# Four-token sums of v on TensorE instead of a second load of v, sums of q on GpSimd, another written order

## The chip, the core and the metric

The kernel runs on one core of a Trainium2 chip. A core has a matrix engine (TensorE, PE in the profile, PEld for its weight loads), VectorE (DVE), ScalarE (ACT), GpSimd (POOL), a queue engine (SyncE, SP) that issues most DMAs, and 16 DMA engines. The metric is the device time of one execution in microseconds; the median of several runs counts.

## The reference

An attention of two parts over q, k, v of shape (8 batches, 8 heads, 576 tokens, 64), all fp32, is followed by a mixture of 8 experts with one expert per token. Cut to what matters:

```python
q_d = q.reshape(B, H, Sd, 4, D).mean(axis=3)      # the same for k_d and v_d; Sd = 144
out_up = np.repeat(sm_attn(q_d, k_d, v_d), 4, axis=2)
mask = np.abs(pos[:, None] - pos[None, :]) < 4
out_local = softmax(where(mask, q k^T / 8, -1e9)) @ v
x = (out_up + out_local) as (4608 tokens, 512)
e_idx = argmax(x @ w_gate + modality_bias[modality_id]); gate_w = its softmax value
out[t] = gate_w[t] * (relu(x[t] @ w1[e]) @ w2[e])
```

So v is needed twice: as it is, in windows around each query (local part), and summed over four tokens (the part here called downsampled).

## The kernel before

The attention works on pairs of heads: iteration n = 4 b + hp is batch b and pair hp, 32 iterations in all, two heads on the two halves of the 128 partitions. For each n, TensorE transposes q and k (`tpq`, `tpk`, `tpt`, all tagged "T" in a ring of three PSUM banks), ScalarE and VectorE copy them to `qT` and `kT`, and the four-token sums are made along the free dimension: k by two adds on GpSimd (`d`, `kd`), q by one reduction on VectorE (`qd`, L301). `sc` is the local scores (48 small matmuls of 24 queries by 32 keys, four side by side), `scd` the downsampled scores. VectorE takes maxima (`lm`, `dm`), ScalarE exponentiates (`exp`, `de`), GpSimd scales (`nl`, `nd`). The local weights are transposed on VectorE and placed in `Pw`; the downsampled ones are transposed on TensorE (`pdt`) with the 144 keys in two halves of 72, and copied to `PdT`. `avl` and `avd` multiply by v, and `X` adds both.

Two loads bring v. `load_v` fills `vw`, in which partition 32 j + x, column (head, k) holds token 96 k + 24 j - 3 + x, x from 0 to 31: windows of 32 tokens at a pitch of 24, for `avl`. `load_vg` (L237) brings the same v again, eight tokens to a partition, 288 KB for each n, into the expert stage's weight buffers (`raw`) for n below 28 and into q's and k's buffers after that; GpSimd's `vt` and `vd_` (L251, L258) add its tokens to `vd`, 72 keys by 2 halves.

After every batch the router multiplies x with the gate weights (`lg`), finds each token's expert, scatters token numbers into a table and stores the rows of x in HBM (`xr`, `R`, `store`). Two units of 256 tokens are computed early, in the attention's tail; then come the last router counts, tables, gathers of rows (`xg`, transposed by `xt`), and some 17 further units of expert matmuls (L844, L891).

The order of all instructions of the attention and the router is written out: `PHASE` gives each step a time in iterations, step f of iteration n gets n + PHASE[f], and the calls are sorted by it and issued in that order on every engine, each of which runs its own in order. Loads stand at times computed from PHASE. When the last scores are through (`free`, L1036), the buffers of q, k and their sums are given back, and the early experts' weights are split in them. Behind that a scheduler sets the order.

Of the kernel before, what the change touches and what calls it, by code (L numbers as in the profile page):

```python
# [75 lines left out]
class Consts:  # L76
    def __init__(s, tc, pool, psum):
        nc = tc.nc

# [12 lines left out]
        m = pool.tile([128, WIN], BF16, name="band")
        nc.gpsimd.memset(m, 0.0)
        for j in range(4):
            t = m[32 * j : 32 * j + 32]
# [2 lines left out]
            nc.gpsimd.affine_select(out=t, in_=t, pattern=[[-1, WIN]], compare_op=ALU.is_ge, fill=NEG, base=6,
                                    channel_multiplier=1)
# [81 lines left out]
class Attention:  # L181


    def __init__(s, tc, ctx, ectx, C, psum, raw, q, k, v):
        s.tc, s.C, s.ps, s.raw = tc, C, psum, raw
# [10 lines left out]
        for j in range(2):
            nc.vector.memset(s.kT[j][:, 0:PAD], 0.0)
            nc.vector.memset(s.kT[j][:, S + PAD :], 0.0)
            nc.vector.memset(s.vw[j][0:32, 0], 0.0)
            nc.vector.memset(s.vw[j][96:128, H * NB - 1], 0.0)  # L200

        for j in range(NPW):
            nc.gpsimd.memset(s.Pw[j], 0.0)
# [33 lines left out]
    def load_vg(s, n):  # L237
        b, hp = divmod(n, 4)
        if n < 28:
            vg = s.raw.tile([128, 1024], F32, name="raw")  # L240
        else:
# [4 lines left out]
    def vt(s, n, i):
        v5 = s.VG.pop(n).rearrange("p h (c t d) -> p (h c) t d", c=2, t=4)
        t = s.t["vt", n] = s.ld.tile([72, 4, 2, D], F32, name="vt", bufs=2)  # L250
        s.nc.gpsimd.tensor_tensor(t, v5[:, :, 0:2], v5[:, :, 2:4], op=ALU.add)  # L251

    def vd_(s, n, i):
        b, hp = divmod(n, 4)
        if hp == 0:
            s.vd[b] = s.wk.tile([72, H, 2, D], F32, name="vd")
        t = s.t.pop(("vt", n))
        s.nc.gpsimd.tensor_tensor(s.vd[b][:, 2 * hp : 2 * hp + 2].rearrange("p h c d -> p (h c) d"), t[:, :, 0],  # L258
                                  t[:, :, 1], op=ALU.add)
# [37 lines left out]

    def qd(s, n, i):

        dd = s.t["qd", n] = s.ld.tile([128, 144], F32, name="qd")  # L300
        s.nc.vector.tensor_reduce(dd, s.t["qT", n].rearrange("m (g t) -> m g t", t=4), op=ALU.add, axis=AX.X)  # L301

    def d(s, n, i):
        d2 = s.t["d", n] = s.ld.tile([128, 144, 2], F32, name="d2", bufs=1)
        T4 = s.kT[n % 2][:, PAD : PAD + S].rearrange("m (g t) -> m g t", t=4)
        s.nc.gpsimd.tensor_tensor(d2, T4[:, :, 0:2], T4[:, :, 2:4], op=ALU.add)

    def kd(s, n, i):
        d2 = s.t.pop(("d", n))
        dd = s.t["kd", n] = s.ld.tile([128, 144], F32, name="kd")  # L310
        s.nc.gpsimd.tensor_tensor(dd.rearrange("m (c g) -> m g c", c=2), d2[:, :, 0].rearrange("m (g c) -> m g c", c=2),
                                  d2[:, :, 1].rearrange("m (g c) -> m g c", c=2), op=ALU.add)
# [67 lines left out]
    def nd(s, n, i):  # L380
        z, e = s.t["zr", n], s.t["de", n]
        s.nc.gpsimd.tensor_tensor(e, e, z[:, 2 * NB :].unsqueeze(2).broadcast_to([128, 3, 144]), op=ALU.mult)
# [12 lines left out]
    def pdt(s, n, kc):  # L395

        p = s.t["pdt", n, kc] = s.ps.tile([72, 512], F32, name="pdt", tag="T", bufs=3)
        for c in range(3):
            s.nc.tensor.transpose(p[:, 128 * c : 128 * c + 128], s.t["de", n][:, c, 72 * kc : 72 * kc + 72], s.C.ident)
# [8 lines left out]
    def avd(s, n, i):  # L408
        b, hp = divmod(n, 4)
        PdT = s.t.pop(("PdT", n))  # L410
        pd = s.t["avd", n] = s.ps.tile([128, 144], F32, name="avd", tag="A", bufs=2)
        for kc in range(2):
            for a in range(2):
                s.nc.tensor.matmul(pd[64 * a : 64 * a + 64, :], s.vd[b][:, 2 * hp + a, kc, :], PdT[:, kc, a, :],
# [489 lines left out]
def build(tc, q, k, v, mid, w_gate, bias, w1, w2, out):  # L904
    nc = tc.nc
    with ExitStack() as ctx:
# [8 lines left out]
        with ExitStack() as actx:  # L915
# [47 lines left out]
            for nm, p in P.items():  # L963
# [199 lines left out]
```

## Time and profile before

| | |
|---|---|
| median of 3 runs | 773.27 us (770.15 to 775.43) |
| profiled run | 774.68 us, span 773.0 us |
| TensorE busy | 702.1 us, 91% of the span |
| VectorE, ScalarE, GpSimd busy | 473.6, 433.2, 327.3 us |
| granted TensorE clock, mean | 0.937 |
| moved by DMA | 150.97 MB |

The span falls into the attention (to about 310 us), a tail in which early experts run beside the last iterations, and the expert stage up to 773 us. In rows of instruction groups, "x" is followed by a count, then come the busy time in us, the mean length of one in ns, and the idle time of the engine just ahead of them with what ended it; "issue" there means that no wait in the profile explains it. In rows of waits stand the total in us, how often, and the longest. In rows of windows, each engine has its busy time and number of instructions, then come the granted clock as a share of the full one, the mean busy share of the DMA engines and GB/s. A matmul of fp32 data shows as two rows.

### The profile page before, as it was taken

The page shows a single profiled execution, that of the slowest core. Times are in us where ns is not written, and L with a number is a line of the kernel's source. Part 1 is how long each engine was busy: PE and PEld are TensorE (multiplying, and loading weights), DVE is VectorE, ACT ScalarE, POOL GpSimd, SP SyncE. Part 2 cuts the span into 40 slices and gives each one's busy share as a digit, 9 for nine tenths or more (in the row PEclk, how much of TensorE's full clock was granted, in tenths as well). Part 3 has the DMA queues.
Part 4 walks back from the last instruction along what each step waited for, and adds up shares of the span by engine and source line. Part 5 has one row for each costly group of instructions (what it writes and reads, how often), then busy time and mean ns, then how long its engine had stood idle before and what let it go on. Part 6 is the DMA issues. An engine that isn't in the chain of part 4 may idle for free. (4 is left out here: it accounts for less than half of the span.)

```text
span 773.0 us, 20639 instructions
## 1 busy us (share of the span) xinstructions
PE 702.1 (91%) x8243; PEld 609.7 (79%) x8243; DVE 473.6 (61%) x924; ACT 433.2 (56%) x908; POOL 327.3 (42%) x369
## 2 busy tenths in 40 slices
PE   5879989877979888989799999999999999999995
PEld 3757767766767767777788999898999889999894
DVE  4666877847677867676576565555565555665620
ACT  2556768756746667754565455555455545465620
POOL 6554758666646796114543332232332333221101
PEclk8788989989888889999799999999999999999998
DMA  9999999999798654366897676666666666766500
GB/s 187 153 181 206 207 189 197 180 208 195 149 181 146 175 104 145 122 234 208 286 314 248 225 246 219 232 215 220 234 227 235 217 216 210 245 216 225 186 14 18
DMA packets 206436, 150.97 MB, mean 195 GB/s; under 512 B 134045, under 2 KB 172993, under 8 KB 206338
## 3 DMA queue, kind: packets, MB, share of 16 engines
q1 hardware_dynamic: 198082, 130.40, 66.7%
q0 software_dynamic: 8256, 19.22, 7.8%
q8 instruction: 66, 1.08, 0.6%
q14 instruction: 32, 0.26, 0.2%
HBM read 130.38 MB, written 19.47 MB: 194 GB/s over the span
## 5 line engine op out<-in xcount | busy, mean ns | idle before, releaser
L777 DVE TENSOR_TENSOR wlo<-raw,whi 128x1024 fp32r<-128x1024 f32 x130 | 159.2, 1233 | 135.2 <-ACT whi L771 134.2
L771 ACT CAST whi<-raw 128x1024 fp32r<-128x1024 f32 x130 | 135.6, 1049 | 126.3 <-PE l L844 59.5
L844 PE MATMUL l<-xh,whi 128*128 128x256 f32 x488 | 138.8, 286 | 2.2 <-DVE hl L847 1.5
L844 PE MATMUL l<-xh,wlo 128*128 128x256 f32 x488 | 139.1, 285 | 0.4 <-DVE wlo L777 0.4
L844 PE MATMUL l<-xl,whi 128*128 128x256 f32 x488 | 138.9, 285 | 0.0
L895 POOL DMA_INDIRECT out_dram<-o,tg x37 | 41.0, 1108 | 170.0 <-ACT o L894 141.9
L891 PE MATMUL l<-whi,hl 128*128 128x512 f32 x256 | 100.4, 394 | 0.0
L891 PE MATMUL l<-wlo,hh 128*128 128x512 f32 x256 | 100.0, 392 | 0.0
L891 PE MATMUL l<-whi,hh 128*128 128x512 f32 x256 | 98.1, 397 | 0.0
L844 PEld LDWEIGHTS l<-xh,whi 128*128 128x128 f32 x488 | 93.7, 193 | 4.1 <-DVE hl L847 2.0
L844 PEld LDWEIGHTS l<-xh,wlo 128*128 128x128 f32 x488 | 93.5, 192 | 1.3 <-DVE wlo L777 0.6
L844 PEld LDWEIGHTS l<-xl,whi 128*128 128x128 f32 x488 | 93.4, 191 | 1.0 <-issue 0.5
L790 POOL DMA_INDIRECT tg<-tab,midx x33 | 41.0, 1243 | 74.8 <-DMA out_dram<-o,tg 68.7
L847 DVE SCALAR_TENSOR_TENSOR hl<-l,hh 128x512 fp32r<-128x512 f32 x72 | 49.3, 686 | 24.0 <-ACT hh L846 24.0
L800 POOL DMA_INDIRECT xg<-xs,tg x37 | 42.6, 1151 | 50.6 <-DMA tg<-tab,midx 26.2
L585 POOL DMA_INDIRECT tab<-ig,si x36 | 36.9, 1025 | 57.5 <-DVE mbase L693 31.6
L846 ACT ACTIVATE hh<-l 128x512 fp32r<-128x512 f32 x72 | 42.6, 594 | 30.4 <-PE l L844 30.4
L891 PEld LDWEIGHTS l<-wlo,hh 128*128 128x128 f32 x256 | 48.1, 188 | 10.8
L429 PE MATMUL avl<-Pw,vw 128*64 128x96 f32 x768 | 50.2, 289 | 7.0 <-issue 7.0
L891 PEld LDWEIGHTS l<-whi,hh 128*128 128x128 f32 x256 | 48.1, 188 | 10.2
L393 ACT COPY Pw<-lt 32x288 f32<-32x288 f32 x128 | 55.0, 429 | 2.0
L891 PEld LDWEIGHTS l<-whi,hl 128*128 128x128 f32 x256 | 48.2, 188 | 10.1
(211 smaller groups left out, 1416.8 us busy)
## 6 DMA issues: line engine op xcount, KB each, us to landing
raw<-in_moe_w_dram SPq DMA_DIRECT2D x152, 512.0 KB
vw<-in_v_dram SPq DMA_DIRECT2D x53, 192.0 KB
xs<-R SPq DMA_DIRECT2D x36, 256.0 KB
qt<-in_q_dram SPq DMA_DIRECT2D x30, 288.0 KB
kt<-in_k_dram SPq DMA_DIRECT2D x30, 288.0 KB
raw<-in_v_dram SPq DMA_DIRECT2D x28, 288.0 KB
vw<-in_v_dram SPq DMA_DIRECT2D x15, 96.0 KB
xg<-xs,tg POOLq DMA_INDIRECT x37, 4.9
```

Of the source, the lines that this page charges most:

```text
L393: s.nc.scalar.copy(s.Pw[n % NPW][r, :, j, :SUB], s.t["lt", n][r, :, :SUB])
L429: s.nc.tensor.matmul(p[64 * a : 64 * a + 64, c], vw[:, NB * (4 * (hp // 2) + hp % 2 + 2 * a) + k, :], Pw[:, NB * a + k], start=True, stop= ...
L585: i = nc.gpsimd.indirect_dma_start(out=s.tab[:, :], out_offset=bass.IndirectOffsetOnAxis(ap=C.si[:, t : t + 1], axis=0), in_=C.ig[:, t, :] ...
L771: nc.scalar.copy(hi, raw)
L777: nc.vector.tensor_tensor(lo, raw, hi.bitcast(F32), op=ALU.subtract)
L790: nc.gpsimd.indirect_dma_start(out=T[:, h, :], out_offset=None, in_=s.tab[:, :], in_offset=bass.IndirectOffsetOnAxis(ap=idx[:, u, h : h + ...
L800: s.gathered = nc.gpsimd.indirect_dma_start(out=R[:, h, :], out_offset=None, in_=s.xs[:n, :], in_offset=bass.IndirectOffsetOnAxis(ap=T[:, ...
L844: nc.tensor.matmul(p[:, f, :], a[:, k, fs], x[:, k, :], start=(k == 0 and i == 0), stop=(k == 3 and i == 2))
L846: nc.scalar.activation(hh[:, 2 * c : 2 * c + 2, :], p, AF.Relu)
L847: nc.vector.scalar_tensor_tensor(hl[:, 2 * c : 2 * c + 2, :], p, 0.0, hh[:, 2 * c : 2 * c + 2, :].bitcast(F32), op0=ALU.max, op1=ALU.subtract)
L891: nc.tensor.matmul(p, a[:, f, hs], x[:, f % 2, :], start=(f == 0 and i == 0), stop=(f == 7 and i == 2))
L895: nc.gpsimd.indirect_dma_start(out=s.out[:, :], out_offset=bass.IndirectOffsetOnAxis(ap=T[:, h, 0:1], axis=0), in_=o, in_offset=None, boun ...
```

## The change

The second load of v, and GpSimd's sums of it, are gone. In their place `vp` multiplies the blocks of keys in `vw` by a constant matrix `pool` (128 by 32) that picks the 24 middle tokens of each window and adds them by four, six sums for each of the four j. It runs once for two iterations: 2 x 3 matmuls with 256 columns (4 heads by 64), each into 32 partitions of a PSUM bank from the ring "T", three side by side. VectorE copies the result, 96 by 512, to `vd` (`vc`). Six sums stand in every 24 + 8 = 32 partitions, so the downsampled keys now come in an order by k and j with eight empty places in each 32; `de` is written in 24 of every 32 columns of three buffers that were zeroed at the start, and `pdt`, `PdT`, `avd` work on 96 in place of 72 keys. The sums of q are made by two adds on GpSimd (`qe`, `qd`), as those of k are. `PHASE` has new numbers throughout; a line of it is shown. `free` no longer waits for `vd`.

```diff
 PHASE = {
-    "tpk": 0.8507, "tpt": 0.9279, "kT0": 0.9467, "qT1": 1.0813, "kT1": 1.1757, "d": 1.4154, "kd": 1.4303,
+    "tpk": 0.0000, "tpt": 0.0000, "kT0": 0.0720, "tpq": 0.0893, "qT1": 0.3475, "kT1": 0.4026, "qT0": 0.4377,
...
+        s.pool = pool.tile([128, 32], F32, name="pool")
+        nc.gpsimd.memset(s.pool, 0.0)
+        for j in range(4):
+            t = s.pool[32 * j : 32 * j + 32, 6 * j : 6 * j + 6]
+            nc.gpsimd.memset(t, 1.0)
+            nc.gpsimd.affine_select(out=t, in_=t, pattern=[[-4, 6]], compare_op=ALU.is_ge, fill=0.0, base=-PAD,
+                                    channel_multiplier=1)
+            nc.gpsimd.affine_select(out=t, in_=t, pattern=[[4, 6]], compare_op=ALU.is_ge, fill=0.0, base=PAD + 3,
+                                    channel_multiplier=-1)
...
+        s.De = [s.one.tile([128, 3, 32 * NB], F32, name=f"de{j}") for j in range(3)]
...
+        for j in range(3):
+            nc.gpsimd.memset(s.De[j], 0.0)
...
-    def load_vg(s, n):
...
-        s.nc.sync.dma_start(vg, s.v[b].rearrange("(f a g) (p t) d -> f g p a (t d)", f=2, a=2, t=8)[hp // 2, hp % 2])
-    def vt(s, n, i):
...
-    def vd_(s, n, i):
...
+    def vp(s, n, i):
+        b, hp = divmod(n, 4)
+        vw = s.vw[b % 2].rearrange("p (h k) d -> p k h d", k=NB)
+        p = s.t["vp", n // 2] = s.ps.tile([96, 2, 4, D], F32, name="vp", tag="T", bufs=3)
+        for kc in range(2):
+            for j in range(3):
+                s.nc.tensor.matmul(p[32 * j : 32 * j + 32, kc], s.C.pool, vw[:, 3 * kc + j, 2 * hp : 2 * hp + 4],
+                                   start=True, stop=True, skip_group_check=True, tile_position=(0, 32 * j))
+    def vc(s, n, i):
+        t = s.t["vd", n // 2] = s.wk.tile([96, 2, 4, D], F32, name="vd")
+        s.nc.vector.tensor_copy(t, s.t.pop(("vp", n // 2)))
...
+    def halves(s, nm, n, T):
+        d2 = s.t[nm, n] = s.ld.tile([128, 144, 2], F32, name=nm, bufs=1)
+        T4 = T.rearrange("m (g t) -> m g t", t=4)
+        s.nc.gpsimd.tensor_tensor(d2, T4[:, :, 0:2], T4[:, :, 2:4], op=ALU.add)
+    def whole(s, nm, n, d2):
+        dd = s.t[nm, n] = s.ld.tile([128, 144], F32, name=nm)
+        s.nc.gpsimd.tensor_tensor(dd, d2[:, :, 0], d2[:, :, 1], op=ALU.add)
+    def qe(s, n, i):
+        s.halves("qe", n, s.t["qT", n])
     def qd(s, n, i):
-        dd = s.t["qd", n] = s.ld.tile([128, 144], F32, name="qd")
-        s.nc.vector.tensor_reduce(dd, s.t["qT", n].rearrange("m (g t) -> m g t", t=4), op=ALU.add, axis=AX.X)
+        s.whole("qd", n, s.t.pop(("qe", n)))
...
-            s.nc.tensor.transpose(p[:, 128 * c : 128 * c + 128], s.t["de", n][:, c, 72 * kc : 72 * kc + 72], s.C.ident)
+            s.nc.tensor.transpose(p[:, 128 * c : 128 * c + 128], s.t["de", n][:, c, 96 * kc : 96 * kc + 96], s.C.ident)
...
-                s.nc.tensor.matmul(pd[64 * a : 64 * a + 64, :], s.vd[b][:, 2 * hp + a, kc, :], PdT[:, kc, a, :],
+                s.nc.tensor.matmul(pd[64 * a : 64 * a + 64, :], vd[:, kc, n % 2 + 2 * a, :], PdT[:, kc, a, :],
...
-                    for n in range(N):
+                    for n in range(0, N, 2 if f in ("vp", "vc") else 1):
...
-            for n in range(4, N):
-                call(max(n - 4 + P["vt"] + 0.25, 2 * (n // 2) - 1 + last + 0.25 if n >= 28 else 0), at.load_vg, n)
...
-            free = N - 1 + max(P["scd"], P["sc0"], P["sc1"], P["vd"]) + 0.02
+            free = N - 1 + max(P["scd"], P["sc0"], P["sc1"]) + 0.02
```

More of the change, by code (lines that the diff above doesn't have):

```diff
@@ L181, with __init__ @@
 class Attention:
-    def __init__(s, tc, ctx, ectx, C, psum, raw, q, k, v):
-        s.tc, s.C, s.ps, s.raw = tc, C, psum, raw
+    def __init__(s, tc, ctx, ectx, C, psum, q, k, v):
+        s.tc, s.C, s.ps = tc, C, psum
         nc = s.nc = tc.nc
@@ L191, in __init__ @@
         s.one = ctx.enter_context(tc.tile_pool(name="aone", bufs=1, reuse_waits="tile"))
-        s.QK, s.VG, s.vd, s.t = {}, {}, {}, {}
+        s.QK, s.t = {}, {}
         s.vw = [(s.ld, s.one)[j].tile([128, H * NB, D], F32, name=f"vw{j}", bufs=1) for j in range(2)]
@@ L235, in load_v @@
                               vf[lo + n0 * BLK : lo + n1 * BLK].rearrange("(n x) d -> x n d", x=BLK)[:32])
-    def load_vg(s, n):
+    def vp(s, n, i):
         b, hp = divmod(n, 4)
[L239 to L243, printed above, removed]
-        s.nc.sync.dma_start(vg, s.v[b].rearrange("(f a g) (p t) d -> f g p a (t d)", f=2, a=2, t=8)[hp // 2, hp % 2])
-    def vt(s, n, i):
-        v5 = s.VG.pop(n).rearrange("p h (c t d) -> p (h c) t d", c=2, t=4)
-        t = s.t["vt", n] = s.ld.tile([72, 4, 2, D], F32, name="vt", bufs=2)
-        s.nc.gpsimd.tensor_tensor(t, v5[:, :, 0:2], v5[:, :, 2:4], op=ALU.add)
-    def vd_(s, n, i):
[L254 to L259, printed above, removed]
+        vw = s.vw[b % 2].rearrange("p (h k) d -> p k h d", k=NB)
[7 more added lines that the diff above has]
+        s.nc.vector.tensor_copy(t, s.t.pop(("vp", n // 2)))
     def tp(s, n, nm):
@@ L296, in kT_ @@
             s.nc.vector.tensor_copy(kT[:, PAD + 64 * g : PAD + 64 * g + 512], s.t.pop(("tp", "k", n)))
+    def halves(s, nm, n, T):
[7 more added lines that the diff above has]
+        s.halves("qe", n, s.t["qT", n])
     def qd(s, n, i):
-        dd = s.t["qd", n] = s.ld.tile([128, 144], F32, name="qd")
-        s.nc.vector.tensor_reduce(dd, s.t["qT", n].rearrange("m (g t) -> m g t", t=4), op=ALU.add, axis=AX.X)
+        s.whole("qd", n, s.t.pop(("qe", n)))
     def d(s, n, i):
-        d2 = s.t["d", n] = s.ld.tile([128, 144, 2], F32, name="d2", bufs=1)
-        T4 = s.kT[n % 2][:, PAD : PAD + S].rearrange("m (g t) -> m g t", t=4)
-        s.nc.gpsimd.tensor_tensor(d2, T4[:, :, 0:2], T4[:, :, 2:4], op=ALU.add)
+        s.halves("d", n, s.kT[n % 2][:, PAD : PAD + S])
     def kd(s, n, i):
[L309 to L312, printed above, removed]
+        s.whole("kd", n, s.t.pop(("d", n)))
     def mk(s, n, a):
@@ L357, in dm @@
         s.nc.vector.tensor_reduce(m, s.t["scd", n], op=ALU.max, axis=AX.X, negate=True)
-        s.t["de", n] = s.wk.tile([128, 3, 144], F32, name="de", bufs=3)
+        s.t["de", n] = s.De[n % 3]
         s.t["z", n] = s.wk.tile([128, 5, 4], F32, name="z")
@@ L363, in de @@
         m = s.t["dm", n]
-        s.nc.scalar.activation(s.t["de", n][:, c], s.t["scd", n][:, c], AF.Exp, bias=m[:, c : c + 1],
+        x = s.t["de", n][:, c].rearrange("p (k x) -> p k x", k=NB)[:, :, :SUB]
+        s.nc.scalar.activation(x, s.t["scd", n][:, c].rearrange("p (k x) -> p k x", k=NB), AF.Exp, bias=m[:, c : c + 1],
                                accum_out=s.t["z", n][:, 4, c : c + 1])
@@ L380, in nd @@
     def nd(s, n, i):
-        z, e = s.t["zr", n], s.t["de", n]
-        s.nc.gpsimd.tensor_tensor(e, e, z[:, 2 * NB :].unsqueeze(2).broadcast_to([128, 3, 144]), op=ALU.mult)
+        z, e = s.t["zr", n], s.t["de", n].rearrange("p c (k x) -> p c k x", k=NB)[:, :, :, :SUB]
+        s.nc.gpsimd.tensor_tensor(e, e, z[:, 2 * NB :].unsqueeze(2).unsqueeze(3).broadcast_to([128, 3, NB, SUB]),
+                                  op=ALU.mult)
     def lt(s, n, i):
@@ L395, in pdt @@
     def pdt(s, n, kc):
-        p = s.t["pdt", n, kc] = s.ps.tile([72, 512], F32, name="pdt", tag="T", bufs=3)
+        p = s.t["pdt", n, kc] = s.ps.tile([96, 512], F32, name="pdt", tag="T", bufs=3)
         for c in range(3):
-            s.nc.tensor.transpose(p[:, 128 * c : 128 * c + 128], s.t["de", n][:, c, 72 * kc : 72 * kc + 72], s.C.ident)
+            s.nc.tensor.transpose(p[:, 128 * c : 128 * c + 128], s.t["de", n][:, c, 96 * kc : 96 * kc + 96], s.C.ident)
     def PdT(s, n, kc):
         if ("PdT", n) not in s.t:
-            s.t["PdT", n] = s.wk.tile([72, 2, 2, 144], F32, name="PdT")
+            s.t["PdT", n] = s.wk.tile([96, 2, 2, 144], F32, name="PdT")
         src = s.t.pop(("pdt", n, kc))[:, :408].rearrange("p (c x) -> p c x", c=3)[:, :, :128]
@@ L408, in avd @@
     def avd(s, n, i):
-        b, hp = divmod(n, 4)
-        PdT = s.t.pop(("PdT", n))
+        PdT, vd = s.t.pop(("PdT", n)), s.t["vd", n // 2]
         pd = s.t["avd", n] = s.ps.tile([128, 144], F32, name="avd", tag="A", bufs=2)
@@ L920, in build @@
             moe.xg = xg
-            at = Attention(tc, actx, ectx, C, ps, moe.wr, q, k, v)
+            at = Attention(tc, actx, ectx, C, ps, q, k, v)
             at.load_qk(0, 0)
-            at.load_vg(0)
             at.load_v(0, 0, 2)
@@ L926, in build @@
             at.load_qk(0, 1)
-            at.load_vg(1)
             at.load_v(0, 4, 2)
             at.load_v(0, 6, 2)
-            at.load_vg(2)
             at.load_qk(1, 0)
-            at.load_vg(3)
             ro.rp, ro.nr = at.wk, NR
@@ L956, in build @@
             P = PHASE
-            parts = {"kT": "kT_", "Pw": "Pw_", "vd": "vd_", "W": "store"}
+            parts = {"kT": "kT_", "Pw": "Pw_", "W": "store"}
             last = max(P["tpq"], P["tpk"], P["tpt"])
```

20 rows, old and new, of the table PHASE are left out of this document.

## The prediction

> **What bounds the kernel now.** I read the span by stretches first: the start, the attention, its tail, the expert stage.
>
> ```profile
> core 0: us, PE busy (x) PEld busy (x) DVE busy (x) ACT busy (x) POOL busy (x), PEclk, DMA share, GB/s
> 0.00:25.00 25.00, 15.40 (x260) 10.08 (x261) 9.81 (x43) 5.79 (x18) 13.60 (x36) 0.78 1.12 186
> 25.00:310.00 285.00, 242.15 (x5091) 198.40 (x5090) 203.93 (x568) 187.68 (x576) 185.13 (x223) 0.88 0.92 175
> 345.00:773.00 428.00, 411.14 (x2634) 373.52 (x2634) 234.59 (x264) 215.29 (x276) 125.38 (x108) 0.98 0.63 210
> ```
>
> From 25 to 310 us TensorE is busy 85% (242.15 of 285) and the next engine, VectorE, 72%. TensorE sets the attention's pace, but it loses time in two ways: it is idle for 42.85 us, and its granted clock is 0.88, so those 242.15 us hold about 242.15 x 0.88 = 213 us of work at full clock and 29 us of slowness. The expert stage after 345 us is TensorE almost without a gap, and the change doesn't touch it. So the question is what happens to three numbers: 213 of work, 43 of idling, 29 of slowness.
>
> Next, what TensorE waited for in that stretch, and in its later part alone (second block, 190 to 310 us).
>
> ```profile
> PE sc L325 <- issue: 8.1, 6, 3.0
> PE avd L414 <- issue: 8.0, 2, 4.5
> PE avl L429 <- issue: 7.0, 5, 3.3
> PE scd L352 <- DVE qd L301: 5.6, 4, 2.2
> PE pr L541 <- DVE oh L521: 2.6, 2, 1.8
> ```
> ```profile
> PE sc L325 <- issue: 4.9, 4, 2.6
> PE avl L429 <- issue: 2.0, 1, 2.0
> ```
>
> The three rows that end in "issue" sum to 23.1 us in 13 stalls: no semaphore, and in the middle of a group of equal matmuls. The timeline has the longest:
>
> ```profile
> 157.63 1.03 PE L325 MATMUL sc<-kT,qT 64*24 64x32 f32 x96
> 158.59 0.34 PE L414 MATMUL avd<-PdT,vd 72*64 72x144 f32 x1
> 163.41 1.23 PE L414 MATMUL avd<-PdT,vd 72*64 72x144 f32 x7 [4.49 <-issue]
> ```
>
> The first of eight rows runs, the other seven wait 4.49 us, right after 96 rows of sc went through in 1.03 us. I read this as TensorE running out of instructions, which come by DMA:
>
> ```profile
> PE 702.1 (91%) x8243; PEld 609.7 (79%) x8243; DVE 473.6 (61%) x924; ACT 433.2 (56%) x908; POOL 327.3 (42%) x369
> q8 instruction: 66, 1.08, 0.6%
> raw<-in_v_dram SPq DMA_DIRECT2D x28, 288.0 KB
> ```
>
> Queue q8 moves 66 packets of 1.08 MB / 66 = 16.4 KB, one for each 250 of TensorE's 16486 matmuls and weight loads. That they are late because the loads crowd the DMA engines is an inference. For it speaks that the issue waits are 23.1 - 6.9 = 16.2 us in the 165 us up to 190 (9.8 per 100 us) and 6.9 in the 120 us behind it (5.8 per 100 us), while DMA is less busy there:
>
> ```profile
> 25.00:190.00 165.00, 140.60 (x3127) 115.67 (x3126) 117.86 (x330) 111.64 (x350) 102.38 (x127) 0.90 1.08 191
> 190.00:310.00 120.00, 101.55 (x1964) 82.74 (x1964) 86.07 (x238) 76.03 (x227) 82.75 (x97) 0.84 0.71 152
> ```
>
> The Trainium skill, "Runtime: NRT & Kernel Launch", Instruction fetch mechanics, says that the sequencer refills in 16 KiB blocks of 256 instructions by its own DMA queue, and that crossing a block is "mostly hidden". The block size agrees with q8; the hiding does not agree with 23.1 us. By the page's hiding the change would win nothing here, and the sum below would be 7 us longer.
>
> The slowness follows the stalls:
>
> ```profile
> 120.00:140.00 20.00, 19.28 (x439) 15.76 (x439) 14.94 (x43) 16.00 (x52) 16.09 (x21) 1.00 1.00 203
> 140.00:160.00 20.00, 15.88 (x435) 13.07 (x434) 16.50 (x48) 14.55 (x45) 15.34 (x19) 1.00 1.03 192
> 160.00:180.00 20.00, 16.46 (x262) 13.33 (x261) 10.09 (x31) 11.79 (x36) 8.75 (x12) 0.83 1.08 211
> ```
>
> The clock is full for 40 us and 0.83 in the slice that begins inside the 4.49 us stall: a loss of 0.17 x 20 = 3.4 us on top of the stall.
>
> **The change part by part.** TensorE's order, the cycle of one head pair (sc, scd: scores; avd, avl: values; pdt, tp, tpt: transposes; vp is the new sum of v). Before:
>
> ```order
> L325 MATMUL sc<-kT_155,qT 24x32 x48
> L414 MATMUL avd<-PdT,vd 64x144 x4
> L352 MATMUL scd<-kd,qd 64x144 x6
> L429 MATMUL avl<-Pw_158,vw_153 64x96 x12
> L399 MATMUL pdt<-ident,de 72x128 x3
> L266 MATMUL tp<-ident,qt 128x128 x4
> L399 MATMUL pdt<-ident,de 72x128 x3
> ```
>
> After, in the same place of a cycle with vp:
>
> ```order
> L287 MATMUL tpt<-ident,kt 128x64
> L273 MATMUL tp<-ident,qt 128x128 x4
> L338 MATMUL sc<-kT_170,qT 24x32 x48
> L365 MATMUL scd<-kd,qd 64x144 x6
> L428 MATMUL avd<-PdT,vd 64x144 x4
> L261 MATMUL vp<-vw_167,pool 32x256 x6
> L443 MATMUL avl<-Pw_172,vw_167 64x96 x12
> L414 MATMUL pdt<-ident,de_176 96x128 x6
> ```
>
> vp stands in every second cycle, 16 times in all; scd moved ahead of avd, and q's transposes moved ahead of sc.
>
> *Added on TensorE.* vp is six matmuls with 256 columns, three to a bank side by side in 32-column tiles. The nearest row is the router's lg, eight of them, four side by side, in a slice at full clock:
>
> ```profile
> 132.33 1.07 PE L476 MATMUL lg<-X,wg 128*32 128x256 f32 x16
> L476 PE MATMUL lg<-X,wg x128: 379/432/523, 66.3 to 324.6; 128*32 128x256 f32 x64, 128*32 128x320 f32 x64
> ```
>
> vp has 12 such rows for 16: between 1.07 x 12/16 = 0.80 us and, with two groups like lg, 1.07 us. I take 1.0, nearer the second: +16 us (13 to 17). The transposes pdt take 96 columns of weights for 72:
>
> ```profile
> L399 PEld LDWEIGHTS pdt<-ident,de 128*72 128x72 f32 x184 | 20.0, 125 | 6.9 <-POOL de L382 2.5 <-issue 1.3
> L266 PEld LDWEIGHTS tp<-ident,kt 128*128 128x128 f32 x116 | 13.4, 147 | 5.0 <-ACT PdT L406 3.0 <-ACT R L574 1.2 <-issue 0.4
> ```
>
> Between 125 ns and the 147 of 128 columns: at most 192 x 22 ns = 4 us, under matmuls in part; +1.
>
> *Removed on VectorE, moved on GpSimd.* GpSimd's order, two cycles before and two after (le and de are scaled here; d, qe are half sums, kd, qd whole ones; vt, vd the removed sums of v):
>
> ```order
> L378 TENSOR_TENSOR le<-le,zr 128x384
> L382 TENSOR_TENSOR de<-de,zr 128x432
> L251 TENSOR_TENSOR vt<-raw 72x512
> L258 TENSOR_TENSOR vd<-vt 72x256
> L306 TENSOR_TENSOR d_814<-kT_155 128x288
> L311 TENSOR_TENSOR kd<-d_814 128x72x2
> ```
>
> ```order
> L392 TENSOR_TENSOR le<-le,zr 128x384
> L396 TENSOR_TENSOR de_175<-de_175,zr 128x18x24
> L309 TENSOR_TENSOR d<-kT_170 128x288
> L309 TENSOR_TENSOR qe<-qT 128x288
> L313 TENSOR_TENSOR kd<-d 128x144
> L313 TENSOR_TENSOR qd<-qe 128x144
> ```
>
> Two sums of v went, two of q came, of the same size as those of k.
>
> ```profile
> L251 POOL TENSOR_TENSOR vt<-raw 72x512 f32<-72x512 f32 x27 | 34.2, 1268 | 0.0
> L258 POOL TENSOR_TENSOR vd<-vt 72x256 f32<-72x256 f32 x30 | 23.0, 766 | 1.6
> L306 POOL TENSOR_TENSOR d<-kT 128x288 f32<-128x288 f32 x29 | 20.2, 697 | 1.8 <-ACT kT L294 1.8
> L311 POOL TENSOR_TENSOR kd<-d 128x144 f32<-128x144 f32 x29 | 13.0, 449 | 2.0
> L301 DVE TENSOR_REDUCE qd<-qT 128x144 f32<-128x576 f32 x30 | 22.2, 739 | 6.1 <-ACT qT L289 6.0
> L296 DVE COPY kT<-tp 128x512 f32<-128x512 f32 x29 | 19.9, 685 | 12.1 <-PE tp L266 12.1
> ```
>
> GpSimd: 1268 + 766 out, 697 + 449 in: 0.89 us less a cycle. VectorE: 739 out, and per pair of cycles one copy vp to vd of 512 columns, by the kT row 685: 0.40 less a cycle. The 5.6 us that scd waited for VectorE's qd go; what is late next is qd on GpSimd, behind de and d. I credit -4 (0 to -5.6). The new wait blocks avd, vp and avl behind scd on TensorE. The other idling, 42.85 - 23.1 - 5.6 = 14 us, is mostly single waits for VectorE and ScalarE; with VectorE lighter and TensorE half a microsecond longer per cycle, they are met less often: -4 (from +3, if vp, which takes one of the three transposes' banks every second cycle, makes them wait for ScalarE, to -10).
>
> *Removed on the DMA queues.* The second load of v, 32 issues of 288 KB on SP's queue, 28 of them the raw row above. With fewer bytes queued, I take the later part's rate for the whole stretch: 285 x 5.8/100 = 16 us of issue waits for 23: -7 (+4 to -15). Below that stands the order itself: sc's burst, now followed by vp, still empties the instruction store.
>
> *Clock.* Idling falls from 42.85 to 42.85 - 7 - 4 - 4 = 28. In proportion, and for 230 us of work in place of 213, slowness is 29 x 28/42.85 x 230/213 = 20: -8 (+5 to -20).
>
> *Start.*
>
> ```profile
> 20.36 0.88 PE L266 MATMUL tp<-ident,kt 128*128 128x128 f32 x3 [6.68 <-DMA kt<-in_k_dram]
> L203 POOL MEMSET Pw<- x3: 1047/1057/1057, 3.0 to 5.7; 128x1152 f32 x3
> 2.82 0.20 POOL L98 TENSOR_SCALAR_AFFINE_SELECT band<-band 32x32 bf16<-32x32 bf16 x1
> ```
>
> One 288 KB load of v stood ahead of that k; at the first row's 186 GB/s it is 1.6 us: -1.6 (0 to -3). GpSimd's three new memsets, half as long as those of Pw (1.6 us), and twelve steps that make the constant (0.2 us each, 2.4) hide in the 6.68 us; uncovered they would cost 4.
>
> *Tail.* The attention's buffers are given back about a cycle earlier, and 23 more first-layer expert matmuls stand on TensorE ahead of the last router counts, 120 for 97. At 411.14/2634 = 0.156 us a matmul (window from 345 us) that is 3.6 us, if the counts wait for them. Behind the counts comes the chain of tables and row gathers, for which TensorE waits at its end:
>
> ```profile
> PE xt L822 <- DMA xg<-xs,tg: 6.0, 2, 5.4
> ```
>
> The early weights' splitting starts a cycle earlier too: +1 (-2 to +4).
>
> *Sum:* 16 + 1 - 4 - 4 - 7 - 8 - 1.6 + 1 = -6.6. The profiled run took 774.68 us, 1.4 over the median of 773.27; the sum gives 768.1 for it, 767 for the median.
>
> **The rivals.** *The vp work isn't paid back (slower).* TensorE is the bound, its burst before avl gets longer, and instructions go on coming late as the shorter cycle offers DMA the same load per microsecond. Then idling stays and vp is paid at clock 0.88: 17/0.88 = 19, less the start: 773.3 + 19 - 1.6 = 791. It decides once issue waits stay at 23 us. For it: 85% busy; against it: the later part's rate. 0.22. The Trainium skill's hiding of instruction fetches (Runtime: NRT & Kernel Launch, as above), under which the stalls have another cause than DMA, would lead here.
>
> *The stalls go.* Issue waits fall to 6 and the clock to 0.96: slowness 230 x 0.04 = 9, so -20, issue -17: 16 + 1 - 4 - 4 - 17 - 20 - 1.6 + 1 = -28.6, 745. For it: the 40 us at clock 1.00 above; against it: DMA was as busy there. 0.17.
>
> *Transposes cool the clock (slower).* The new order has pdt, tp, tpt, tp in one run. The Trainium skill, "TensorE: Matmul & The Clock Gate", Part 4, says transposes don't count as busy for the gate. In rows: one 3.4 us loss in each of two router cycles of seven batches, 48 us less my 7: 814. Against it: 120 to 160 us holds such runs at clock 1.00. 0.04.
>
> *It doesn't do what it says:* the tiles of vp don't overlap, 12 x 0.432 = 5.2 us each, 16 x 4.2 = 67 more than my sum: 834. The lg row speaks against it. 0.02.
>
> **How the numbers follow.** My forecast has 0.55, its own range 756 to 779 from the bounds of issue, clock and waits. A measurement of this kernel tells about 1% from no change, 765.5 to 781. The forecast lies near that line: 0.26 of it is faster, 0.29 inside. With the stalls gone, 0.17 more: faster 0.43, same 0.29, slower 0.22 + 0.04 + 0.02 = 0.28. The range goes to 746 below, which leaves out half of the second rival (0.08), and to 790 above, which leaves out half of the first (0.11).
>
> **What would show it.** vp busy near 1 us each and side by side; no TensorE wait on qd; issue rows near 16 us between 25 us and the attention's end; clock there near 0.91; the last scd near 295 us where it was 302.8:
>
> ```profile
> L352 PE MATMUL scd<-kd,qd x384: 280/283/500, 10.6 to 302.8; 64*64 64x144 f32 x192
> ```
>
> If issue rows stay over 23 us or GpSimd's qd takes their place, the forecast is wrong.

## The result, and the profile after

The changed kernel takes 751.81 us (median of 4 runs, 747.42 to 754.67); the kernel before took 771.71 us beside it (4 runs, 769.87 to 775.43). The ratio is 0.973, with a 95% interval of 0.966 to 0.980: 2.7% faster. On two other chips it was 0.981 (0.973 to 0.990) and 0.982 (0.973 to 0.990), with medians of 757.17 and 761.51 us. In ratios and mean differences, here and below, executions more than 1.5% above a kernel's fastest are left out; medians and ranges are over all of them.

The profiled run after the change took 754.67 us, 20.0 less than the profiled one before. Windows of both, from 25 us to the start of the last scd, which was at 302.8 us before and is at 280.0 now (columns as in the prediction's windows):

```profile
25.00:302.80 277.80, 234.95 (x5019) 192.04 (x5019) 200.64 (x560) 182.96 (x562) 179.44 (x217) 0.87 0.94 178
```
```profile
25.00:280.00 255.00, 235.65 (x5189) 181.31 (x5183) 175.97 (x545) 179.48 (x561) 147.31 (x215) 0.94 0.80 156
L365 PE MATMUL scd<-kd,qd x384: 279/283/500, 12.5 to 280.0; 64*64 64x144 f32 x192
345.00:753.00 408.00, 392.10 (x2525) 358.18 (x2523) 222.53 (x233) 209.15 (x269) 110.50 (x99) 0.98 0.65 213
```

TensorE is busy for the same time, but at clock 0.94 for 0.87. In the terms of the prediction: work at full clock went from 234.95 x 0.87 = 204.4 to 235.65 x 0.94 = 221.5 us (+17.1), idling from 42.85 to 19.35 (-23.5), slowness from 30.5 to 14.1 (-16.4). The split between work and slowness holds to a few us only: the two control runs of the same kernel below give 223.0 and 223.4 us of work. The sum is -22.8 us at the last scd, and from there to the end the new span is 2.8 us longer (753.0 - 280.0 = 473.0 for 773.0 - 302.8 = 470.2).

TensorE's waits between 25 and 295 us after the change:

```profile
PE scd L365 <- POOL qd L313: 6.0, 2, 5.4
PE scd L365 <- issue: 4.2, 3, 2.2
PE sc L338 <- issue: 2.6, 3, 1.4
PE pdt L414 <- POOL de L396: 1.6, 4, 0.9
PE avl L443 <- ACT Od L433: 1.4, 2, 0.8
```

The rows in "issue" sum to 6.8 us in 6 stalls, for 23.1 in 13. The wait for VectorE's qd (5.6) is gone, but a wait for GpSimd's qd stands in its place, nearly all of it one stall. The timeline shows vp as it was sized, and that stall (TensorE's rows, then GpSimd's):

```profile
53.82 1.06 PE L261 MATMUL vp<-vw,pool 128*32 128x256 f32 x12
54.82 1.21 PE L443 MATMUL avl<-Pw,vw 128*64 128x96 f32 x24
225.48 1.71 PE L365 MATMUL scd<-kd,qd 64*64 64x144 f32 x12 [5.36 <-POOL qd L313]
```
```profile
218.62 0.68 POOL L309 TENSOR_TENSOR qe<-qT 128x288 f32<-128x288 f32 x1
223.62 0.98 POOL L804 DMA_INDIRECT tg<-tab,eidx  x1 [4.33 <-DMA tab<-ig,si]
224.61 0.44 POOL L313 TENSOR_TENSOR kd<-d 128x144 f32<-128x144 f32 x1
224.99 0.44 POOL L313 TENSOR_TENSOR qd<-qe 128x144 f32<-128x144 f32 x1
```

From the start of vp to the next instruction it is 1.00 us. GpSimd has qe ready at 219.3 us, but the first gather of table entries (`tg`) stands next in its order, waits until the scatter into that table (`tab`) has landed, and kd and qd wait behind it.

### The profile page after: what moved, and what is told of

Its sections match the earlier page's. It is cut to its first block, busy times and chain, and to the rows that moved or that the text cites. A ratio compares the mean times of both kernels' runs of the same rounds, so it can differ in the third digit from the quotient of the medians.

```text
span 753.0 us, 21037 instructions
## 1 busy us (share of the span) xinstructions
PE 705.5 (94%) x8435; PEld 602.7 (80%) x8435; DVE 450.4 (60%) x908; ACT 429.3 (57%) x908; POOL 293.1 (39%) x385
## 5 line engine op out<-in xcount | busy, mean ns | idle before, releaser
L858 PE MATMUL l<-xl,whi 128*128 128x256 f32 x488 | 140.7, 289 | 0.0
L804 POOL DMA_INDIRECT tg<-tab,midx x33 | 37.8, 1145 | 72.8 <-DMA out_dram<-o,tg 66.7
L392 POOL TENSOR_TENSOR le<-le,zr 128x384 f32<-128x384 f32 x32 | 26.7, 834 | 91.5 <-DVE zr L388 72.9
L814 POOL DMA_INDIRECT xg<-xs,tg x37 | 40.8, 1102 | 53.0 <-DMA tg<-tab,midx 35.2
```

The lines of the kernel that those rows point to most:

```text
L392: s.nc.gpsimd.tensor_tensor(e, e, z[:, : 2 * NB].unsqueeze(2).broadcast_to([128, 2 * NB, WIN]), op=ALU.mult)
L804: nc.gpsimd.indirect_dma_start(out=T[:, h, :], out_offset=None, in_=s.tab[:, :], in_offset=bass.IndirectOffsetOnAxis(ap=idx[:, u, h : h + ...
L814: s.gathered = nc.gpsimd.indirect_dma_start(out=R[:, h, :], out_offset=None, in_=s.xs[:n, :], in_offset=bass.IndirectOffsetOnAxis(ap=T[:, ...
L858: nc.tensor.matmul(p[:, f, :], a[:, k, fs], x[:, k, :], start=(k == 0 and i == 0), stop=(k == 3 and i == 2))
```

## The experiments

Each is the kernel after (or before, where it says so) with one edit. The profile of each run but the second of the old order gives one row below, from its own window between 25 us and its last scd: idling is that window less TensorE's busy time, slowness is busy time x (1 - clock); the waits are those between 25 and 300 us.

| kernel | last scd | idling | of it issue (stalls) | longest wait | clock | slowness | median |
|---|---|---|---|---|---|---|---|
| before | 302.8 | 42.9 | 23.1 (13) | 4.5 | 0.87 | 30.5 | 771.7 |
| after | 280.0 | 19.4 | 6.8 (6) | 5.4 | 0.94 | 14.1 | 751.8 |
| after, control 1 | 281.7 | 22.0 | 12.7 (22) | 5.0 | 0.95 | 11.7 | 757.2 |
| after, control 2 | 279.8 | 22.1 | 11.6 (16) | 5.9 | 0.96 | 9.3 | 761.5 |
| loads put back once | 291.0 | 25.2 | 15.6 (16) | 5.4 | 0.93 | 16.9 | 774.9 |
| loads put back, again | 301.1 | 28.5 | 19.6 (27) | 5.8 | 0.91 | 22.3 | 777.3 |
| before, load cut to 1/8 | 287.0 | 35.9 | 16.9 (16) | 3.1 | 0.92 | 18.1 | 762.2 |
| gathers later | 283.8 | 21.6 | 8.8 (8) | 7.6 | 0.93 | 16.6 | 759.6 |
| old order | 289.8 | 27.8 | 11.2 (12) | 4.2 | 0.94 | 14.2 | 763.0 |
| q's sums on VectorE | 289.3 | 25.5 | 14.3 (12) | 3.2 | 0.93 | 16.7 | 762.6 |
| vp twice | 296.3 | 21.4 | 13.6 (20) | 4.2 | 0.94 | 15.0 | 769.4 |
| gathers spread out | 274.3 | 18.6 | 11.9 (19) | 3.1 | 0.97 | 6.9 | 753.7 |
| gathers early | 274.2 | 19.6 | 14.9 (22) | 2.1 | 0.99 | 2.3 | 751.9 |

They were timed on three chips: the first put-back, the cut load, the old order and the gathers placed later (below) on one, where before took 775.2; control 1, the second put-back, vp twice and the spread gathers on another (before 776.5); control 2, the old order again, q's sums on VectorE and the early gathers on a third (before 779.5).

**Is it the load of v?** My theory: the 28 transfers of 288 KB crowd the DMA engines, instructions come late, TensorE stalls, the clock falls. The rival: the new order and the lighter engines removed the stalls. The loads go into weight buffers of the expert stage, four at the start and one in each further cycle; nothing reads them.

```diff
+    def load_vg(s, n):
+        b, hp = divmod(n, 4)
+        vg = s.raw.tile([128, 1024], F32, name="raw")
+        vg = vg[:72, :1024].rearrange("p (h x) -> p h x", h=2)
+        s.nc.sync.dma_start(vg, s.v[b].rearrange("(f a g) (p t) d -> f g p a (t d)", f=2, a=2, t=8)[hp // 2, hp % 2])
...
+            for n in range(4, 28):
+                call(n - 4 + 2.53, at.load_vg, n)
```

> The changed kernel with the removed transfers back: the 28 middle loads of 288 KB of v are issued again on SP's queue, at the same places of the head-pair cycles and into buffers that stand free; nothing reads them, so no engine gets other work. If DMA load makes TensorE's instructions late (my theory), TensorE's waits that end in issue between 25 and 295 us go from 6.8 us back to 15 to 23, the granted clock there from 0.94 to about 0.89, and the time to 762 to 770. If the written order or the engines' lighter work removed the stalls (rival), issue stays under 9 us, the clock at 0.93 or more, and the time within 3 us of the changed kernel's 752.

The time was 774.9 us, but its 10 runs went from 756.54 to 790.05, those of the kernel before on that chip from 760.56 to 786.26, and the changed kernel itself had not run there. The time is over the 762 to 770 expected; the profiled execution, of 766.28 us, has 15.6 us of issue waits and clock 0.93. So I repeated it beside a control.

> The changed kernel itself, unchanged, beside the next three on one chip. The runs that put the load back, took it away from the kernel before and used the old order stood on a chip on which the changed kernel had not run, and there the kernel before spread from 760 to 786 us. Expected here: 750 to 760 and a spread of a few us; if it spreads as widely as the kernel before does, the earlier comparisons can't be read by their medians.

> The changed kernel with the removed loads of v issued again, a second time, now beside the changed kernel itself. The first time its runs spread from 757 to 790 with a median of 775, and the profiled one, among its faster, had 15.6 us of issue waits and a clock of 0.93. If DMA load makes instructions late, by a different amount in each execution, the median lies 10 to 25 us over the changed kernel's and the spread is over 10 us. If the first time was the chip's doing, it lies within 4 us of it.

The control took 757.17 us (756.65 to 763.03), the kernel with the loads put back 777.26 (768.31 to 781.17): 16.8 us more in the mean (95% interval of the two means' difference 12.1 to 21.5). Against the kernel before its ratio is 1.004 (0.998 to 1.011). The waits and the window of this run, and below them those of the control:

```profile
PE sc L344 <- issue: 9.2, 12, 2.6
PE avl L449 <- issue: 5.4, 6, 1.9
PE scd L371 <- issue: 5.0, 9, 1.1
25.00:301.10 276.10, 247.64 (x5206) 188.91 (x5201) 176.96 (x548) 180.67 (x562) 149.57 (x219) 0.91 0.95 174
```
```profile
PE sc L338 <- issue: 5.7, 11, 1.3
PE scd L365 <- issue: 4.6, 7, 1.8
PE avl L443 <- issue: 1.8, 2, 1.0
25.00:281.70 256.70, 234.70 (x5189) 180.80 (x5183) 176.43 (x546) 179.07 (x561) 147.30 (x215) 0.95 0.80 155
```

No engine got other work, and yet issue waits are 19.6 us for 12.7, DMA's busy share 0.95 for 0.80, and the clock 0.91 for 0.95. No row has TensorE waiting for a transfer. The loads alone take back the whole gain: with them, everything else in the change is worth nothing in sum that could be measured. The rival falls.

The other side was tried on the kernel before. Its GpSimd sums keep their sizes and read one eighth of the data broadcast, so the sums of v, and with them the downsampled values, are left out:

```diff
-        s.nc.sync.dma_start(vg, s.v[b].rearrange("(f a g) (p t) d -> f g p a (t d)", f=2, a=2, t=8)[hp // 2, hp % 2])
+        s.nc.sync.dma_start(vg[:, :, :D], s.v[b].rearrange("(f a g) (p t) d -> f g p a (t d)", f=2, a=2, t=8)[hp // 2, hp % 2][:, :, :D])
...
+        x = s.VG.pop(n)[:, :, :D].unsqueeze(2).broadcast_to([72, 2, 4, D])
...
-        s.nc.gpsimd.tensor_tensor(t, v5[:, :, 0:2], v5[:, :, 2:4], op=ALU.add)
+        s.nc.gpsimd.tensor_tensor(t.rearrange("p (h c) t d -> p h (c t) d", c=2), x, x, op=ALU.add)
```

> The kernel before, in its own order, with the second load of v cut to one eighth of its bytes (64 of 512 floats of a row; GpSimd's sums read those broadcast, at the same sizes, so the sums over four tokens of v are left out and hold other values). If DMA load makes the instructions late, the issue waits between 25 and 310 us fall from 23.1 us to under 12, the clock rises from 0.88 to 0.92 or more, and the time falls from 773 to 750 to 762, lower still than the load put back costs the changed kernel since vp isn't paid here. If the order made the stalls, issue stays near 23 us and the time at 768 to 774.

```profile
25.00:287.00 262.00, 226.09 (x5015) 184.79 (x5012) 198.15 (x558) 180.95 (x558) 172.77 (x217) 0.92 0.85 157
PE sc L325 <- issue: 6.4, 8, 1.1
PE avd L414 <- issue: 5.4, 2, 3.1
PE avl L429 <- issue: 3.6, 4, 1.1
```

Half a miss: the clock is 0.92 as expected and the time 762.24 us at the edge of what was expected, but issue waits fell only to 16.9 us, not under 12; the ratio to the kernel before is 0.989 (0.979 to 1.000). Queue q1 moves as many packets as before here (198082), since each row stays one packet; only the bytes fell. Whether packets or bytes make the instructions late was not tried apart and stays open. What is shown is that the transfers bring "issue" stalls and the clock loss.

That the mechanism is a late fetch of instructions is borne out by the traces' packet records for most of the longer stalls. Each packet on queue q8 is one block of 16384 bytes. The stall of 4.49 us in the kernel before ends at 163.41 us, 1.43 behind the landing of such a block at 161.98. Of its seven issue stalls of 1 us or more between 25 and 300 us, six end 1.41 to 1.66 us behind a block, and with the loads put back again six of six do (1.44 to 1.62). Over the fourteen profiles 41 of 66 such stalls end 1.3 to 1.7 us behind a block, and only 3 of the 34 stalls that end on a semaphore. The other 25 stay unexplained, three of the four in the kernel after among them. Nor do the blocks themselves take longer with the load (1.24 us in the mean before, 1.26 after), so why they come late is not shown.

**What vp costs.**

```diff
-        for kc in range(2):
+        for kc in (0, 1, 0, 1):
```

> The changed kernel with the six matmuls of vp run twice in each of their 16 places (same result). If TensorE is the bound and vp is a price paid in full, as the prediction has it (1.0 us each), the time rises by 15 to 19 us. If vp lies in TensorE's idle time, or works as cover for a wait, it rises by under 6 us.

It took 769.42 us, 8.9 more in the mean than control 1 (4.2 to 13.7), between the two expectations.

```profile
122.98 1.93 PE L261 MATMUL vp<-vw,pool 128*32 128x256 f32 x24
25.00:296.30 271.30, 249.93 (x5369) 189.09 (x5363) 176.58 (x544) 178.70 (x560) 146.73 (x215) 0.94 0.76 146
```

24 rows take 1.93 us where 12 take 1.06: 0.87 more in each of 16 places, 13.9 in sum, near the lower bound of 0.80 that lg's row gave. By busy time x clock the work rose from 223.0 to 234.9 us, 11.9. So vp is paid, and hardly any of it hides in TensorE's idle time, which is 21.4 for 22.0 us. How much of it reaches the end is less clear: in the profiles the last scd comes 14.6 us later than in control 1 (296.3 for 281.7) and the end 9.1 us later (766.32 for 757.21).

**What the order is worth.** The operations of the kernel after, with the phases of the kernel before; vp and vc stand where vt and vd stood, qe and qd at 1.60 and 1.65:

```diff
 PHASE = {
-    "tpk": 0.0000, "tpt": 0.0000, "kT0": 0.0720, "tpq": 0.0893, "qT1": 0.3475, "kT1": 0.4026, "qT0": 0.4377,
+    "tpk": 0.8507, "tpt": 0.9279, "kT0": 0.9467, "qT1": 1.0813, "kT1": 1.1757, "d": 1.4154, "kd": 1.4303,
...
-            free = N - 1 + max(P["scd"], P["sc0"], P["sc1"]) + 0.02
+            free = N - 1 + max(P["scd"], P["sc0"], P["sc1"], P["vc"]) + 0.02
```

> The changed kernel's operations in the order of the kernel before: its table of phases, with vp and its copy where the removed sums of v stood, and q's two half sums on GpSimd just behind q's transpose copies. No second load of v. If the missing load alone brings the gain, this comes within 4 us of the changed kernel (748 to 756), issue waits 5 to 10 us, clock 0.93 to 0.95. If the new order brings it, the time stays at 765 to 775 with issue waits over 15 us.

The median was 763.03 us, between the two expectations. Its profile has the stall on qd, and waits for PdT of which the kernel after has none on xr or tp:

```profile
PE scd L365 <- POOL qd L313: 4.6, 3, 4.2
PE xr L581 <- ACT PdT L421: 4.2, 8, 1.4
PE tp L273 <- ACT PdT L421: 2.8, 4, 1.4
```

It was repeated beside a control:

> The changed kernel itself again, beside the next three on one chip: 750 to 760 us, and 1.5 to 3% under the kernel before.

> The changed kernel's operations in the order of the kernel before once more, now beside the changed kernel itself: on another chip it took 763 us, with 11.2 us of issue waits between 25 and 300 us, 4.6 us of scd waiting for GpSimd's qd and 7.0 us of xr and tp waiting for ScalarE's PdT. If the new order is worth nothing by itself (the missing load brings the gain), it lies within 4 us of the changed kernel. If the order adds to it, it lies 5 to 12 us over it, by the waits for PdT above all, with issue waits alike (within 5 us).

The control took 761.51 us, a little over the 750 to 760 expected, the old order 765.70: 2.3 us more in the mean, with an interval from -7.1 to +11.7. Its profile, of an execution of 772.32 us, again has 7.0 us of waits for PdT on xr and tp, besides 4.8 for qd and 15.5 in issue. So 7.0 us of waits for ScalarE's PdT are shown to go with the new order, and what that is worth in time isn't settled; by the two intervals it is less than the load.

**The move of q's sums.**

```diff
-    "d": 0.6735, "qe": 0.6981, "mk0": 0.7524, "mk1": 0.9618, "kd": 1.1650, "qd": 1.2004, "sc0": 1.2151, "sc1": 1.2193,
+    "d": 0.6735, "mk0": 0.7524, "mk1": 0.9618, "kd": 1.1650, "qd": 0.6981, "sc0": 1.2151, "sc1": 1.2193,
...
-        s.whole("qd", n, s.t.pop(("qe", n)))
+        dd = s.t["qd", n] = s.ld.tile([128, 144], F32, name="qd")
+        s.nc.vector.tensor_reduce(dd, s.t["qT", n].rearrange("m (g t) -> m g t", t=4), op=ALU.add, axis=AX.X)
```

> The changed kernel with q's sums over four tokens back on VectorE, one reduction a head pair, behind the second transpose copy, where GpSimd's first half sum stood. In the changed kernel scd's one long wait, 5 us, is for a qd that stands on GpSimd behind the gather of table entries; kd stands there too, so that wait stays here, under kd's name (4 to 6 us). VectorE gets 30 reductions of 0.74 us and GpSimd loses 1.1 us a head pair. If the move to GpSimd brought the removed 5.6 us, waits of TensorE for VectorE of 3 to 8 us come back and the time rises by 4 to 12 us; if VectorE has room for the reductions at this place, the time stays within 4 us of the changed kernel's.

It took 762.55 us, 1.8 more than control 2 (-4.5 to +8.2), and no row has scd, sc or avl waiting for VectorE; the stall of scd stays under kd's name, at 3.2 us for the 4 to 6 expected:

```profile
PE scd L366 <- POOL kd L313: 3.2, 1, 3.2
```

At this place in the order VectorE has room for q's sums: the move itself brought nothing that these runs can tell from zero.

**The gather in GpSimd's queue.** The kernel calls `entries` (the gathers `tg`) four times, i from 0 to 3, counted from t, the time just behind the last store of rows (`st`) of the batches whose tokens are worked on early. Three edits move only these calls: later; spread over a cycle behind the next cycle's qd; and all four directly behind that qd.

```diff
-                call(t + 0.5 + 0.6 * i, entries, i // 2, i % 2)
+                call(t + 1.3 + 0.5 * i, entries, i // 2, i % 2)
```
```diff
+                call(t + 1.72 + 0.2 * i, entries, i // 2, i % 2)
```
```diff
+                call(t + 1.72 + 0.03 * i, entries, i // 2, i % 2)
```

> The changed kernel with one step moved: the early gathers from the table of tokens (tg, on GpSimd's queue) are called 0.8 cycles later. In the changed kernel such a gather waits on GpSimd for the table's scatter to land, with kd and qd queued behind it, and TensorE's scd waits 5.36 us for qd at 225 us; behind that the clock drops. If that queueing is the cause, the row of scd waiting for GpSimd's qd falls from 6.0 us to under 1.5, the clock slices behind 225 us recover, and the time falls by 5 to 9 us, to 743 to 747. If qd is late for its own work on GpSimd (rival), the wait stays near 5 us and the time within 2 us of 752.

The qd wait went, but the time was 759.61 us, not 743 to 747 (no control on that chip; 0.986 of the kernel before, 0.975 to 0.996), since the last gather had fallen behind the next batch's scatter and waited for its landing, with le and de queued behind it. GpSimd's rows, TensorE's row, and windows behind that stall:

```profile
246.22 0.96 POOL L804 DMA_INDIRECT tg<-tab,eidx  x1 [6.07 <-DMA tab<-ig,si]
250.04 0.93 POOL L396 TENSOR_TENSOR de<-de,zr 128x432 f32<-128x432 f32 x1
251.02 1.52 PE L414 MATMUL pdt<-ident,de 128*96 128x128 f32 x6 [7.64 <-POOL de L396]
250.00:255.00 5.00, 3.98 (x18) 3.17 (x18) 1.50 (x5) 2.74 (x8) 4.64 (x8) 0.50 0.58 21
255.00:260.00 5.00, 5.00 (x119) 3.90 (x119) 2.34 (x6) 1.46 (x4) 4.44 (x7) 0.50 0.29 90
260.00:265.00 5.00, 5.00 (x45) 4.18 (x44) 1.97 (x5) 3.09 (x12) 4.63 (x7) 0.67 0.44 64
265.00:270.00 5.00, 5.00 (x157) 3.68 (x156) 3.98 (x13) 4.70 (x15) 3.87 (x7) 1.00 0.89 265
```

The clock is halved for over 10 us behind it: 5 x 0.5 + 5 x 0.5 + 5 x 0.33 = 6.7 us lost on top of the 7.64.

> The changed kernel with the four early gathers of table entries placed between two batches' scatters: behind the qd of the second cycle after the first scatter, and all four ahead of the next batch's scatter. Placed later and wider apart the qd wait went (6.0 to 0) but the last gather fell behind the next scatter and TensorE's pdt waited 7.6 us for GpSimd's de. If the queueing of a gather behind a scatter's landing is the cause, both waits are now under 1.5 us, and the time is 4 to 9 us under the changed kernel's. If GpSimd is late by its own work, a wait for qd or de of over 3 us stays and the time is the same.

It took 753.66 us, 6.4 less than control 1 with an interval of -15.3 to +2.5, and a wait of TensorE's pdt for de of 3.14 us stayed, behind the next scatter:

```profile
236.61 1.00 POOL L599 DMA_INDIRECT tab<-ig,si  x1 [4.82 <-DVE dm L370]
```

That the scatter waits for the last gather, as the next expectation has it, is an inference: the row names VectorE's dm, which the scatter doesn't read, and what it does read (`si`) was ready at 233.7 us. So all four gathers went to where GpSimd is idle.

> The changed kernel with the four early gathers one behind the other, directly behind the qd of the second cycle after the first scatter, where GpSimd stood idle from 221 to 224 us with them spread over a cycle. Spread, the last gather was still under way when the next batch's scatter came up, which waited 4.8 us for it, with le and de behind, and TensorE's pdt waited 3.1 us for de. Expected: no wait of TensorE for qd or de over 1.5 us, and a time 5 to 10 us under the changed kernel's (a little under the 3.5 us that the spread gathers gained). If the order behind it takes it back, a wait of some 3 us for de or qd shows at another place and the time is 1 to 4 us under.

```profile
PE sc L338 <- issue: 6.4, 11, 1.5
PE scd L365 <- issue: 4.4, 5, 2.1
PE avl L443 <- issue: 4.1, 6, 1.3
PE tpt L287 <- ACT R L588: 1.1, 1, 1.1
25.00:274.20 249.20, 229.59 (x5187) 175.76 (x5187) 176.31 (x545) 178.59 (x561) 147.59 (x216) 0.99 0.85 160
```

It took 751.90 us beside control 2's 761.51: 8.2 us less in the mean (1.6 to 14.8), 0.970 of the kernel before (0.962 to 0.978). No wait of TensorE for qd or de is over 1.5 us. This one moved call makes a version that beats both kernels. Its idling, 19.6 us, is hardly less than control 2's 22.1; what went is the slowness, 2.3 us for 9.3. No stall of this run's attention is over 2.12 us, where control 2 has one of 5.87 for qd and one of 4.30 in issue, each with half rate behind it. Only the first has to do with the gathers, so part of the difference may be that execution's chance.

## Why the prediction was right

The forecast was faster, 767 us with a range of 746 to 790; it is 751.8. The mechanism was the forecast's: bytes off the DMA queues, fewer issue waits, a better clock, vp paid out of it. The size was not: the terms sum to -6.6 us, and the profiled runs differ by 20.0. It lies between the forecast and the rival in which the stalls go (745), and a range 44 us wide took it in near its lower end. Of the signs that were named, vp's came true; the last scd came at 280.0, not near 295, and a wait on qd stayed. Term by term:

- **vp and pdt, +17:** right. Work at full clock rose by 17.1 us in a window in which the start's gain is already taken off; vp ran side by side, at 1.00 us each.
- **Issue waits, 23 to 16:** right in direction, mis-sized. Three profiles of the kernel after show 6.8, 12.7 and 11.6 us. The step that failed was "I take the later part's rate for the whole stretch"; that part's 5.8 us per 100, at a DMA share of 0.71, was no lower bound. After the change it is 2.5 to 4.6 per 100 us at a share of 0.80 to 0.82, so the share alone doesn't set the rate. 16.9 is what the kernel before shows with an eighth of that load's bytes.
- **The qd wait, -4:** wrong. It came back on GpSimd at 6.0 us in two stalls (5.0 and 5.9 in the controls). I named the condition under which the forecast would be wrong (GpSimd's qd takes its place), but priced qd only "behind de and d". What failed is that I didn't follow GpSimd's queue for the DMAs in it. The gather's wait was there to be read in the kernel before, 4.62 us with vt, vd, d and kd queued behind it:

```profile
245.26 1.00 POOL L790 DMA_INDIRECT tg<-tab,eidx  x1 [4.62 <-DMA tab<-ig,si]
```

  There it cost TensorE nothing: kd stood at 1.43 and scd at 2.10 of the cycle. After the change kd stands at 1.165, qd at 1.200 and scd at 1.224, so the slack between maker and user went from two thirds of a cycle to almost none.
- **Other idling, 14 to 10:** mis-sized in the safe direction. It is 19.35 - 6.8 - 6.0 = 6.5 us, and 22.0 - 12.7 - 5.0 = 4.3 in control 1. The old order with the new operations has 27.8 - 11.2 - 4.6 = 12.0, of which 7.0 are waits for PdT, so the order, more than the lighter VectorE, seems to have removed it.
- **Clock, -8:** mis-sized, -16.4 (0.94 where I gave about 0.91). "In proportion" fits the profiled run only by chance: 30.5 x 19.35/42.85 x 221.5/204.4 = 14.9 for 14.1 measured, but control 2 has 9.3 and the early gathers 2.3 us of slowness with as much idling.
- **Start, -1.6:** right. The wait for k shrank from 6.68 to 4.92 us, and GpSimd's new steps are hidden, since the one wait for its qd there, 1.51 us, ends at 12.5 us, ahead of the wait for k:

```profile
19.29 1.09 PE L273 MATMUL tp<-ident,kt 128*128 128x128 f32 x4 [4.92 <-DMA kt<-in_k_dram]
```

- **Tail, +1 (-2 to +4):** +2.8 us from the last scd to the end. The row gathers wait as before, and an expert matmul that the new order puts ahead waits for the router's last counts:

```profile
PE xt L836 <- DMA xg<-xs,tg: 5.3, 2, 4.2
PE l L858 <- DVE mn L623: 3.7, 1, 3.7
```

The rivals. *vp not paid back (791):* its condition, issue waits that stay at 23 us, didn't hold. With the loads put back they are 19.6 us and the kernel is as fast as before, so that rival describes the change without its main part, and even there it was too dark. *Transposes cool the clock:* 0.94 to 0.99 with the same transposes in a run. *Tiles of vp that don't overlap:* 1.06 us for 12 rows. On the Trainium skill's "mostly hidden" fetch (Runtime: NRT & Kernel Launch, Instruction fetch mechanics): the issue stalls grow with the load, 12.7 to 19.6 us, most of those of 1 us or more in all profiles end just behind a block, and that is not hidden.

## What to carry to other kernels

A load that is off the critical path and whose data arrives in time can still cost the bound engine: here 28 transfers cost TensorE some 17 us through stalls that no semaphore shows and the clock behind them, more than the matmuls that replaced them. When an order is rewritten, look at every DMA on the queue that a step is moved behind, and at the slack between each maker and its user: a gather that waited 4.6 us unnoticed became a stall of 5.4. Don't price idle time by its sum alone: some 20 us of it went with 14.1 us of slowness in one run and 2.3 in another, and stalls over 3 us always cost clock here.

## What the runs showed of the hardware

The sum of idling doesn't set the clock's loss. All 17 stalls of TensorE over 3 us between 25 and 300 us of these profiles, from 3.09 to 7.64 us, had a clock of 0.50 to 0.66 in the 4 us behind them. Shorter ones cost clock in some places and not in others. In the version with early gathers the stalls of 1.08, 1.14, 1.25 and 1.38 us left it at 1.00, and only two, of 1.48 and 2.12 us, moved it: 0.93 in each of these 25 us slices, a loss of 0.07 x 25 = 1.75 us apiece.

```profile
67.70 0.25 PE L338 MATMUL sc<-kT,qT 64*24 64x32 f32 x6 [1.48 <-issue]
85.59 0.65 PE L365 MATMUL scd<-kd,qd 64*64 64x144 f32 x6 [2.12 <-issue]
222.86 1.21 PE L443 MATMUL avl<-Pw,vw 128*64 128x96 f32 x23 [1.25 <-issue]
50.00:75.00 25.00, 23.52 (x483) 17.67 (x470) 17.59 (x55) 16.94 (x55) 13.54 (x21) 0.93 1.02 183
75.00:100.00 25.00, 22.88 (x512) 17.27 (x511) 14.77 (x43) 17.27 (x55) 13.22 (x20) 0.93 1.03 176
200.00:225.00 25.00, 21.98 (x511) 16.67 (x512) 20.63 (x67) 15.35 (x51) 17.22 (x24) 1.00 0.75 149
```

The Trainium skill, "TensorE: Matmul & The Clock Gate", Part 1, gives as the rule no idle gaps of TensorE over about 3.4 us. Here a gap of 1.48 us was enough; what agrees is the cost, since by the page's window of 3.4 us the loss at half rate is 1.7, an estimate, beside the 1.75 measured. There is no sharp limit either. In the kernel after, a stall of 1.12 us was followed by a clock of 0.50 (146 to 148 us), and with the gathers spread out one of 2.04 us left it at 1.00 (46 to 56 us). In control 2 three stalls of 0.35, 0.47 and 0.60 us within 2.5 us were followed by a clock of 0.50. So the busy share over a short stretch seems to decide, which no run here tests by itself.
